# VectorE and ScalarE programs of a decode-attention kernel written as hardware loops

## The chip, the cores and the metric

The kernel runs on one core of a Trainium2 chip. The metric is the device time of one execution in microseconds (us), the median over the runs of a kernel. With each experiment the kernel before was run again on the same chip, in the same rounds. A ratio is the mean time of one kernel's runs over the mean of the other's runs of the same rounds, so it is not quite the ratio of the medians quoted beside it. The rounds ran on several chips; the kernel before took 1281.5 to 1281.8 us (medians) on each, so differences of under 0.3 us between rounds are not read.

In the profile PE stands for TensorE (PEld for its weight loads), DVE for VectorE, ACT for ScalarE, POOL for GpSimd and SP for SyncE; q1, q8 and q14 are queues of the sixteen DMA engines.

## The reference, cut to what matters

One token attends to a cache of 65,536 keys and values in each of eight key/value heads; two query heads share one of them. A small token-mixing network runs beside it, and a gate mixes both results.

```python
# x: [1, 1, 448];  k_cache, v_cache: [1, 8, 65536, 256] bf16, 268 MB each
q = (x @ wq).reshape(1, 1, 16, 256)...
scores = einsum("bhqd,bhkd->bhqk", q, repeat(k_cache, 2)) * 256 ** -0.5
o = einsum("bhqk,bhkd->bhqd", softmax(scores), repeat(v_cache, 2))
a = o.reshape(1, 1, 4096) @ wo
b = ...            # layernorm, outer product with w1, gelu, product with w2: 14 parts
return g * a + (1 - g) * b
```

Each byte of the caches is used once, for two query heads. Reading 537 MB is most of the work.

## The kernel before

Keys and values come in loads of 4 MB, alternately K and V, into a ring of four slots (two for K, two for V). One load holds four chunks of 2048 positions. SyncE issues a load when its slot has been read:

```python
def load(i):
    w, cd = loads[i]                       # ("k", 0), ("k", 1), ("v", 0), ("k", 2), ("v", 1), ...
    slot = slot_of(w, cd)
    if cd >= 2:
        if w == "k": eng.wait_ge(sem_tr, NB * DC * (cd - 1))     # K slot transposed
        else:        eng.wait_ge(sem_pv, DC * (cd - 1))          # V slot multiplied
    eng.dma_start(ring[:, slot]..., cache_src(w, cd)).then_inc(sem_in[slot], 16)
```

For each chunk TensorE transposes K into four PSUM banks, VectorE copies banks 0 and 2 to SBUF and ScalarE banks 1 and 3, TensorE makes scores, ScalarE their exponentials, and TensorE multiplies them with V. TensorE already runs in two hardware loops, with the network's product and the projection of seven heads between them. VectorE and ScalarE are written out (unrolled) over all 256 chunks:

```python
# TensorE
bodies(2, MID)                 # hardware loop, two load pairs per iteration
...                            # product of the network, projection of 7 heads
bodies(MID, NCD)               # a second copy of the same loop body

# VectorE: straight-line code for 256 chunks
for c in range(NC):
    cd, r = divmod(c, DC)
    if c >= KTB: vec.wait_ge(sem_qk, c - KTB + 1)
    if r == 0 and cd >= 2:
        vec.wait_ge(sem_pv, DC * (cd - 1))
        fold(cd - 2)...                            # add the load pair's sums to accs
        if (cd - 1) % (NCPH // DC) == 0: heads_den(...); heads_out(...)
    ...                                            # at MID: the results of the projection
    if c % BODY == 0 and c:
        vec.wait_ge(sem_qk, c)
        vec.tensor_copy(qcur[:, :, :], head_of(c)).then_inc(sem_qa, 16)
    for b in range(0, NB, 2):
        vec.wait_ge(sem_tr, NB * c + b + 1)
        vec.tensor_copy(ktT[:, c % KTB, b, :], kst_b[:, b, :]).then_inc(sem_ev[b], 1)
    ...                                            # 14 parts of the network in the first 19 chunks

# ScalarE: straight-line code for 256 chunks
for c in range(NC + 1):
    ...                                            # waits, two bank copies, one exponential
```

The softmax here doesn't subtract the row's maximum and nothing guards it: scores larger than these inputs give would overflow.

## Time and profile before

| | before |
|---|---|
| median time | 1281.62 us (3 runs, 1281.35 to 1282.36) |
| moved from HBM | 544.22 MB |
| instruction fetches in the span | 21 of 8 KB (q14), 18 of 16 KB (q8) |
| rate, 20 us windows of the steady part | about 433 GB/s |

These are lines of the page of the kernel before: the busy time of the engines; the 40-slice view (DMA in tenths busy, and GB/s); the DMA queues (packets, MB, share of sixteen engines); the chain of waits by engine; two groups of instructions (busy us, mean ns, then idle before and its cause); and the K loads (KB each, us from issue to landing).

```profile
span 1279.3 us, 45177 instructions
...
PE 1041.8 (81%) x20958; PEld 1024.3 (80%) x20958; DVE 425.9 (33%) x808; ACT 535.5 (42%) x786; POOL 0.9 (0%) x7
...
DMA  9999999999999999999999999999999999999996
GB/s 408 411 426 432 430 432 433 429 432 433 431 431 433 430 432 433 430 432 433 430 430 435 429 433 432 430 432 433 429 433 433 428 434 432 430 433 429 430 431 256
...
q1 hardware_dynamic: 21330, 544.22, 99.1%
q8 instruction: 18, 0.29, 0.1%
q14 instruction: 21, 0.17, 0.0%
...
DMA 61%; PE 33%; DVE 3%; issue 2%; ACT 1%; DVEq 0%; ACTq 0%; SPq 0%
...
L602 ACT ACTIVATE ktT<-kst 128x1024 bf16<-128x1024 bf16 x512 | 504.0, 1023 | 704.2 <-PE kst L255 703.6
L255 PE MATMUL kst<-ident,ring 128*128 128x128 f32 x4096 | 623.3, 321 | 209.2 <-DMA ring<-in_A_k_cache_dram 191.6
...
ring<-in_A_k_cache_dram SPq DMA_DIRECT2D x64, 4096.0 KB, 27.8
```

No compute engine is busy throughout (TensorE, the busiest, 81%). A K load takes 27.8 us from issue to landing although 4.19 MB at 433 GB/s need 9.7 us: about two other loads stand before it in the queue, so TensorE may be late without starving the queue.

The chain of waits, in order of time (start, us, what):

```profile
1252.20 22.02 DMA ring<-in_A_v_cache_dram
...
1274.27 0.60 PE acc L288 x16
...
1277.11 0.67 DVE out_b L566
```

TensorE starts its last 16 products only when the last piece of V is complete, at 1274.2 us, and all that follows is serial. The timeline has the same wait (start, us, what, and idle before):

```profile
1274.27 0.58 PE L288 MATMUL acc<-pT,ring 128*128 128x2 bf16 x16 [0.48 <-DMA ring<-in_A_v_cache_dram]
```

TensorE is idle for only 0.48 us there, for it is late itself: it had waited 3.88 us for the last K load, complete at 1254.7 us. What makes one engine end almost ten us after the first ones (their parts of this last piece are complete from 1264.7 us on, the last at 1274.2) is the subject of this study; the prediction below read past it.

Lines of TensorE (transposes) and ScalarE in a steady chunk, from the timeline (start, us, engine, line, what, and idle before), show the cadence of 2.59 us per chunk:

```profile
226.34 1.95 PE L255 MATMUL kst<-ident,ring 128*128 128x128 f32 x16
...
227.51 1.94 ACT L602 ACTIVATE ktT<-kst 128x1024 bf16<-128x1024 bf16 x2 [0.66 <-PE kst L255]
...
228.93 1.95 PE L255 MATMUL kst<-ident,ring 128*128 128x128 f32 x16
```

### The profile page before, as it was taken

How to read it: one execution, taken by the hardware profiler on the slowest of the kernel's cores; microseconds unless marked ns; L12 is line 12 of the kernel's file. 1: busy time of each engine (PE TensorE's matmuls, PEld its weight loads, DVE VectorE, ACT ScalarE, POOL GpSimd, SP SyncE). 2: the span in 40 equal slices, each digit the busy share in tenths (PEclk: the TensorE clock that was granted, in tenths of full speed). 3: DMA queues.
4: the chain of work that ended last, by engine and by line, in shares of the span. 5: the costliest groups of instructions: out<-in, count | busy, mean ns of one | idle time of the engine just before them, and what ended most of it. 6: DMA issues, size and time to landing. Idle time of an engine off the chain costs nothing.

```text
span 1279.3 us, 45177 instructions
## 1 busy us (share of the span) xinstructions
PE 1041.8 (81%) x20958; PEld 1024.3 (80%) x20958; DVE 425.9 (33%) x808; ACT 535.5 (42%) x786; POOL 0.9 (0%) x7
## 2 busy tenths in 40 slices
PE   4788987887877978878878778778788787789887
PEld 4777987887877877878878778778788787787887
DVE  3676332332332322323323223223233232232332
ACT  2454553443443533534434335335344343353452
POOL 0000000000000000000000000000000000000000
PEclk9778876877877777768778677777687786778876
DMA  9999999999999999999999999999999999999996
GB/s 408 411 426 432 430 432 433 429 432 433 431 431 433 430 432 433 430 432 433 430 430 435 429 433 432 430 432 433 429 433 433 428 434 432 430 433 429 430 431 256
DMA packets 21381, 544.70 MB, mean 426 GB/s; under 512 B 2264, under 2 KB 4315, under 8 KB 4702
## 3 DMA queue, kind: packets, MB, share of 16 engines
q1 hardware_dynamic: 21330, 544.22, 99.1%
q8 instruction: 18, 0.29, 0.1%
q14 instruction: 21, 0.17, 0.0%
q10 hardware_dynamic: 12, 0.01, 0.0%
HBM read 544.22 MB, written 0.00 MB: 425 GB/s over the span
## 4 chain that ended last, share of the span: by engine, by line
DMA 61%; PE 33%; DVE 3%; issue 2%; ACT 1%; DVEq 0%; ACTq 0%; SPq 0%
DMA ring<-in_A_k_cache_dram 59%; PE kst L255 25%; PE sps L267 5%; PE acc L288 2%; DMA ring<-in_A_v_cache_dram 2%; DMA b_b<-in_B_b_dram 1%; DVE ktT L534 0%; PE acc L324 0%; ACT zring L587 0%; PE acc L381 0%; DVE zring L462 0%; DVE wtmp L460 0%; DVE zring L466 0%; DVE gu L478 0%; DVE uring L458 0%
## 5 line engine op out<-in xcount | busy, mean ns | idle before, releaser
L602 ACT ACTIVATE ktT<-kst 128x1024 bf16<-128x1024 bf16 x512 | 504.0, 1023 | 704.2 <-PE kst L255 703.6
L255 PE MATMUL kst<-ident,ring 128*128 128x128 f32 x4096 | 623.3, 321 | 209.2 <-DMA ring<-in_A_k_cache_dram 191.6
L255 PEld LDWEIGHTS kst<-ident,ring 128*128 128x128 f32 x4096 | 578.4, 169 | 216.3 <-issue 104.3
L534 DVE COPY ktT<-kst 128x1024 bf16<-128x1024 bf16 x512 | 352.6, 691 | 512.7 <-PE kst L255 495.9
L267 PE MATMUL sps<-qcur,ktT 128*128 128x2 bf16 x8192 | 241.9, 163 | 3.8 <-DVE ktT L534 2.0
L267 PEld LDWEIGHTS sps<-qcur,ktT 128*128 128x128 bf16 x8192 | 238.7, 97 | 7.0 <-issue 2.2
L288 PE MATMUL acc<-pT,ring 128*128 128x2 bf16 x8192 | 228.7, 164 | 6.3 <-issue 5.8
L288 PEld LDWEIGHTS acc<-pT,ring 128*128 128x128 bf16 x8192 | 220.2, 99 | 6.6 <-issue 6.0
L501 DVE TENSOR_TENSOR accs<-accs,acc 128x36 f32<-128x36 f32 x55 | 10.6, 192 | 261.8 <-PE acc L288 261.7
L593 ACT ACTIVATE pT<-sps 128x32 bf16<-128x32 f32 x256 | 52.1, 203 | 6.6 <-PE sps L267 6.6
L275 PE MATMUL acc<-pT,ones_sq 128*128 128x32 bf16 x252 | 15.8, 176 | 0.0
L500 DVE COPY accs<-acc 128x36 f32<-128x36 f32 x8 | 1.6, 195 | 34.0 <-PE acc L288 33.9
L342 PE MATMUL acc<-ones_sq,gu 1*128 1x1 bf16 x42 | 1.3, 161 | 13.2 <-DMA b_b<-in_B_b_dram 13.2
L342 PEld LDWEIGHTS acc<-ones_sq,gu 1*128 1x128 bf16 x42 | 1.2, 99 | 13.2 <-DMA b_b<-in_B_b_dram 13.2
L275 PEld LDWEIGHTS acc<-pT,ones_sq 128*128 128x128 bf16 x252 | 10.7, 96 | 0.0
L587 ACT ACTIVATE zring<-zring 128x448 bf16<-128x448 bf16 x14 | 8.1, 577 | 6.2 <-DVE zring L468 6.1
L460 DVE TENSOR_TENSOR wtmp<-uring 128x448 bf16<-128x448 bf16 x14 | 5.5, 392 | 1.3 <-issue 0.3
L462 DVE TENSOR_TENSOR zring<-wtmp,uring 128x448 bf16<-128x448 bf16 x14 | 5.5, 393 | 1.0
L478 DVE TENSOR_TENSOR gu<-wtmp,zring 128x448 bf16<-128x448 bf16 x14 | 5.5, 392 | 1.0
L466 DVE TENSOR_TENSOR zring<-uring,wtmp 128x448 bf16<-128x448 bf16 x14 | 5.5, 392 | 1.0
L579 ACT ACTIVATE statb<-statb 1x1 bf16<-1x1 bf16 x1 | 0.2, 207 | 13.0 <-DVE statb L432 13.0
L324 PE MATMUL acc<-wo_sb,oTn 128*1 128x448 bf16 x28 | 5.5, 352 | 0.0
(75 smaller groups left out, 73.3 us busy)
## 6 DMA issues: line engine op xcount, KB each, us to landing
ring<-in_A_k_cache_dram SPq DMA_DIRECT2D x64, 4096.0 KB, 27.8
ring<-in_A_v_cache_dram SPq DMA_DIRECT2D x63, 4096.0 KB, 32.7
wo_sb<-in_A_wo_dram SPq DMA_DIRECT2D x8, 448.0 KB, 25.0
wo_sb<-in_A_wq_dram SPq DMA_DIRECT2D x1, 3072.0 KB, 19.2
ring<-in_A_v_cache_dram SPq DMA_DIRECT2D x1, 2048.0 KB, 18.4
ring<-in_A_v_cache_dram SPq DMA_DIRECT2D x1, 1024.0 KB, 20.5
ring<-in_A_v_cache_dram SPq DMA_DIRECT2D x2, 512.0 KB, 21.6
wo_sb<-in_A_wq_dram SPq DMA_DIRECT2D x1, 512.0 KB, 20.0
```

What stands on the lines that cost most here:

```text
L255: ins = pe.transpose(kst[:, b, j * P:(j + 1) * P], ring_f[:, slot, r * NT + 4 * b + j, :], ident[:, :])
L267: ins = pe.matmul(sps[:, par, 2 * nt:2 * nt + 2], ktT[:, par, b, ntl * DH + dj:(ntl + 1) * DH:2], qcur[:, dj, :], start=(dj == 0), stop=(d ...
L275: ins = pe.matmul(dst[:, DENC:NACC], ones_sq[:, :], pT[:, DC * par + r, :], start=(r == 0), stop=(r == DC - 1))
L288: ins = pe.matmul(acc[:, par, col:col + REP], ring[:, slot_of("v", par), n, dj:DH:2], pT[:, DC * par + r, 2 * nt:2 * nt + 2], start=(last ...
L324: ins = pe.matmul(dst[0:1, PRC:PRC + DM], oTn[:, g, j:j + 1], wo_sb[:, g, hh, dj * DM:(dj + 1) * DM], start=(first and hh == 0 and dj == 0 ...
L460: vec.tensor_tensor(W, U, U, op=ALU.mult)
L462: vec.tensor_tensor(Z, W, U, op=ALU.mult)
L501: return vec.tensor_tensor(dst, dst, src, op=ALU.add)
L534: vec.tensor_copy(ktT[:, c % KTB, b, :], kst_b[:, b, :]).then_inc(sem_ev[b], 1)
L587: act.activation(zring[:, slot, :], zring[:, slot, :], AF.Tanh).then_inc(s_tanh, 1)
L593: act.activation(pT[:, c % PTB, :], sps[:, c % 2, 0:2 * NT], AF.Exp, scale=scale).then_inc(sem_exp, 1)
L602: act.activation(ktT[:, c % KTB, b, :], kst_b[:, b, :], AF.Copy).then_inc(sem_ev[b], 1)
```

## The change

The intent is a smaller program: VectorE runs a loop over the heads with a loop over pairs of load pairs inside it, ScalarE a loop over eight chunks. Waits compare with register values, and head slices are addressed by register. To make the body the same in each iteration, one accumulator is cleared after each head instead of two in turn; the transposes get one semaphore per bank; a head is finished after the load pair, not ahead of its copies; and at the projection TensorE waits for VectorE's reading of the accumulator bank.

```diff
-            for c in range(NC):                    # VectorE
-                ...
+            for cd in range(0, HL, 2):             # first head, with the network: written out
+                pair(DC * cd, per_chunk=early)
+            pair(NCPH, next_head=1)
+            finish_head(0)
+            with nc.Fori(1, H - 1, 1, engines=on) as g:
+                with nc.Fori(0, 3, 1, engines=on) as m:
+                    pair(vec.snap(g * NCPH + m * BODY + BODY, ...))
+                pair(vec.snap(g * NCPH + NCPH, ...), next_head=g + 1)
+                finish_head(g)
+            ...                                    # results of the projection
+            with nc.Fori(DC * MID, NC, BODY, engines=on) as c0:
+                pair(c0)
...
-            for c in range(NC + 1):                # ScalarE
-                ...
+            for c in range(HEAD):                  # 24 chunks written out
+                chunk(c % BODY, c)
+                ...
+            with nc.Fori(HEAD, NC, BODY, engines=OrderedEngineSet([act.engine])) as c0:
+                for k in range(BODY):
+                    chunk(k, c0 + k)
...
-            pe.wait_ge(s_fold, 2)                  # TensorE, at the projection
+            pe.wait_ge(s_brow, 1)
             for g in range(H - 1):
-                ins = project(acc[:, 0, :], g, g == 0, g == H - 2)
+                ins = project(acc[:, 1, :], g, g == 0, g == H - 2)
             ins.then_inc(s_proj, 1)
+            pe.wait_ge(s_brow, 2)
```

As compiled, VectorE's program shrinks from 86,144 to 39,808 bytes and ScalarE's from 84,608 to 13,696. TensorE's stays at 281 KB.

More of the change, by code (lines that the diff above doesn't have):

```diff
@@ L76, in bass_gated_mix__gqa_block_cached__mixer_token_mlp__decode_kernel @@
     MID = NCD - 6
-    assert B0 + FT + 4 < DC * MID and MID >= (H - 1) * NCPH // DC + 2 and MID % 2 == 0
+    assert B0 + FT + 4 < DC * MID and MID == (H - 1) * NCPH // DC + 2
+    assert B0 + FT + 2 <= NCPH
     POC = 0
@@ L118, in bass_gated_mix__gqa_block_cached__mixer_token_mlp__decode_kernel @@
         oTn = sb([P, H, 2 * REP], bf16, "oTn")
-        accs = sb([P, 2, NACC], f32, "accs")
+        accs = sb([P, NACC], f32, "accs")
         part = sb([P, 2, REP], f32, "part")
-        rden = sb([P, 2, 2], f32, "rden")
-        densum = sb([P, 2, 2], f32, "densum")
+        rden = sb([P, REP], f32, "rden")
+        densum = sb([P, REP], f32, "densum")
         xrow_b = sb([1, DM], bf16, "xrow_b")
@@ L156, in bass_gated_mix__gqa_block_cached__mixer_token_mlp__decode_kernel @@
         sem_ident = new_sem("sem_ident")
-        sem_tr = new_sem("sem_tr")
+        sem_tr = [new_sem("sem_tr%d" % b) for b in range(NB)]
         sem_ev = [new_sem("sem_ev%d" % b) for b in range(NB)]
@@ L175, in bass_gated_mix__gqa_block_cached__mixer_token_mlp__decode_kernel @@
         s_bmm = new_sem("s_bmm")
-        s_fold = new_sem("s_fold")
+        s_brow = new_sem("s_brow")
         s_den = new_sem("s_den")
@@ L203, in load @@
                     if w == "k":
-                        eng.wait_ge(sem_tr, NB * DC * (cd - 1))
+                        eng.wait_ge(sem_tr[NB - 1], DC * (cd - 1))
                     else:
@@ L256, in transposes @@
                                            ring_f[:, slot, r * NT + 4 * b + j, :], ident[:, :])
-                    ins.then_inc(sem_tr, 1)
+                    ins.then_inc(sem_tr[b], 1)
             def scores(r, c):
@@ L378, in _ @@
             pe.wait_ge(s_pb, FT)
-            pe.wait_ge(s_fold, 1)
+            pe.wait_ge(sem_acc[1], 16 * (MID // 2))
             for kt in range(FT):
@@ L478, in b_partB, with heads_den @@
                 vec.tensor_tensor(gu[:, kt, :], W, TT, op=ALU.mult).then_inc(s_pb, 1)
-            def heads_den(g):
+            def heads_den():
                 vec.drain()
-                vec.reduce_sum(densum[:, g % 2, :],
-                               accs[:, g % 2, DENC:NACC].rearrange("p (nn hh) -> p hh nn", hh=REP),
+                vec.reduce_sum(densum[:, :], accs[:, DENC:NACC].rearrange("p (nn hh) -> p hh nn", hh=REP),
                                axis=AX.X)
                 vec.drain()
-                vec.reciprocal(rden[:, g % 2, :], densum[:, g % 2, :])
@@ L488, in heads_out @@
-            def heads_out(g):
-                po_v = accs[:, g % 2, POC:POC + 2 * REP].rearrange("p (dj hh) -> p dj hh", dj=2, hh=REP)
-                o_v = oTn[:, g, :].rearrange("p (dj hh) -> p dj hh", dj=2, hh=REP)
-                r_v = rden[:, g % 2:g % 2 + 1, :].broadcast_to((P, 2, REP))
-                vec.drain()
-                vec.tensor_tensor(o_v, po_v, r_v, op=ALU.mult).then_inc(s_oTn, 1)
-            def fold(cd):
-                g, k = divmod(cd, NCPH // DC)
-                vec.drain()
-                dst, src = accs[:, g % 2, :], acc[:, cd % 2, 0:NACC]
-                if k == 0:
-                    return vec.tensor_copy(dst, src)
-                return vec.tensor_tensor(dst, dst, src, op=ALU.add)
@@ L503, in head_of @@
-            def head_of(c):
-                return qT[:, :, REP * (c // NCPH):REP * (c // NCPH) + REP]
-            for c in range(NC):
-                cd, r = divmod(c, DC)
-                if c >= KTB:
-                    vec.wait_ge(sem_qk, c - KTB + 1)
-                if r == 0 and cd >= 2:
-                    vec.wait_ge(sem_pv, DC * (cd - 1))
-                    held = cd - 2 in (MID - 3, MID - 2)
-                    fold(cd - 2).then_inc(s_fold if held else sem_acc[cd % 2], 1 if held else 16)
-                    if (cd - 1) % (NCPH // DC) == 0:
-                        heads_den((cd - 2) // (NCPH // DC))
-                        heads_out((cd - 2) // (NCPH // DC))
-                if r == 0 and cd == MID:
-                    vec.wait_ge(s_bmm, 1)
-                    vec.tensor_copy(brow1[:, :], acc[0:1, 1, PRC:PRC + DM]).then_inc(sem_acc[1], 16)
-                    vec.drain()
-                    vec.tensor_scalar(brow[:, :], brow1[:, :], stat[:, 5:6], None, op0=ALU.add)
-                    vec.drain()
-                    vec.tensor_scalar(run[:, :], brow[:, :], stat[:, 6:7], None, op0=ALU.mult)
-                    vec.wait_ge(s_proj, 1)
-                    vec.drain()
-                    vec.scalar_tensor_tensor(run[:, :], acc[0:1, 0, PRC:PRC + DM], stat[:, 4:5],
-                                             run[:, :], op0=ALU.mult, op1=ALU.add).then_inc(sem_acc[0], 16)
-                if c % BODY == 0 and c:
-                    vec.wait_ge(sem_qk, c)
-                    vec.tensor_copy(qcur[:, :, :], head_of(c)).then_inc(sem_qa, 16)
-                for b in range(0, NB, 2):
-                    vec.wait_ge(sem_tr, NB * c + b + 1)
-                    vec.tensor_copy(ktT[:, c % KTB, b, :], kst_b[:, b, :]).then_inc(sem_ev[b], 1)
@@ new lines, in heads_den, with by_head, fold @@
+                vec.reciprocal(rden[:, :], densum[:, :])
+                vec.drain()
+            def by_head(out_v):
+                po_v = accs[:, POC:DENC].rearrange("p (dj hh) -> p dj hh", dj=2, hh=REP)
+                r_v = rden[:, :].rearrange("p (o hh) -> p o hh", o=1).broadcast_to((P, 2, REP))
+                return vec.tensor_tensor(out_v, po_v, r_v, op=ALU.mult)
+            def fold(par):
+                vec.drain()
+                return vec.tensor_tensor(accs[:, :], accs[:, :], acc[:, par, 0:NACC], op=ALU.add)
@@ new lines, in evacuate, with pair @@
+            def evacuate(r, c):
+                if not isinstance(c, int) or c >= KTB:
+                    vec.wait_ge(sem_qk, c - 1)
+                for b in range(0, NB, 2):
+                    vec.wait_ge(sem_tr[b], c + 1)
+                    vec.tensor_copy(ktT[:, r % KTB, b, :], kst_b[:, b, :]).then_inc(sem_ev[b], 1)
+            def pair(c0, next_head=None, per_chunk=None):
+                for par in range(2):
+                    if not isinstance(c0, int) or c0 >= BODY:
+                        vec.wait_ge(sem_pv, c0 + DC * par - DC)
+                        fold(par).then_inc(sem_acc[par], 16)
+                    if par == 0 and next_head is not None:
+                        vec.wait_ge(sem_qk, c0)
+                        vec.tensor_copy(qcur[:, :, :], qT[:, :, bass.ds(next_head * REP, REP)]
+                                        ).then_inc(sem_qa, 16)
+                    elif par == 0 and (not isinstance(c0, int) or c0):
+                        vec.sem_inc(sem_qa, 16)
+                    for r in range(DC):
+                        c = c0 + DC * par + r
+                        evacuate(r, c)
+                        if per_chunk is not None:
+                            per_chunk(c)
@@ L535, in _, with finish_head, early @@
+            def finish_head(g):
+                heads_den()
+                by_head(oTn[:, bass.ds(g, 1), :].rearrange("p o (dj hh) -> p (o dj) hh", hh=REP)
+                        ).then_inc(s_oTn, 1)
+                vec.drain()
+                vec.memset(accs[:, :], 0.0)
+            def early(c):
                 if c == 1:
@@ L538, in _ @@
                     vec.drain()
-                    vec.tensor_copy(qcur[:, :, :], head_of(0)).then_inc(sem_qa, 16)
+                    vec.tensor_copy(qcur[:, :, :], qT[:, :, 0:REP]).then_inc(sem_qa, 16)
                     vec.wait_ge(s_h, 1)
@@ L546, in _ @@
                     b_partA(c - B0)
-            g = (H - 1) % 2
+            vec.memset(accs[:, :], 0.0)
+            HL = NCPH // DC
+            on = OrderedEngineSet([vec.engine])
+            for cd in range(0, HL, 2):
[4 more added lines that the diff above has]
+                with nc.Fori(0, 3, 1, engines=on) as m:
+                    pair(vec.snap(g * NCPH + m * BODY + BODY, min_val=BODY, max_val=NC))
+                pair(vec.snap(g * NCPH + NCPH, min_val=BODY, max_val=NC), next_head=g + 1)
+                finish_head(g)
+            vec.wait_ge(s_bmm, 1)
+            vec.tensor_copy(brow1[:, :], acc[0:1, 1, PRC:PRC + DM]).then_inc(s_brow, 1)
+            vec.drain()
+            vec.tensor_scalar(brow[:, :], brow1[:, :], stat[:, 5:6], None, op0=ALU.add)
+            vec.drain()
+            vec.tensor_scalar(run[:, :], brow[:, :], stat[:, 6:7], None, op0=ALU.mult)
+            vec.wait_ge(s_proj, 1)
+            vec.drain()
+            vec.scalar_tensor_tensor(run[:, :], acc[0:1, 1, PRC:PRC + DM], stat[:, 4:5],
+                                     run[:, :], op0=ALU.mult, op1=ALU.add).then_inc(s_brow, 1)
+            with nc.Fori(DC * MID, NC, BODY, engines=on) as c0:
+                pair(c0)
             vec.wait_ge(sem_pv, NC - DC)
-            fold(NCD - 2)
+            fold(0)
             vec.wait_ge(s_den, 1)
             vec.drain()
-            vec.tensor_tensor(accs[:, g, DENC:NACC], accs[:, g, DENC:NACC], sps[:, 0, DENC:NACC], op=ALU.add)
-            heads_den(H - 1)
-            po_v = accs[:, g, POC:DENC].rearrange("p (dj hh) -> p dj hh", dj=2, hh=REP)
-            vec.drain()
-            vec.tensor_tensor(part[:, :, :], po_v, rden[:, g:g + 1, :].broadcast_to((P, 2, REP)), op=ALU.mult)
+            vec.tensor_tensor(accs[:, DENC:NACC], accs[:, DENC:NACC], sps[:, 0, DENC:NACC], op=ALU.add)
+            heads_den()
+            by_head(part[:, :, :])
             vec.wait_ge(sem_pv, NC)
@@ L560, in _ @@
                 ins = vec.scalar_tensor_tensor(oTn[:, H - 1, hh:2 * REP:REP], acc[:, 1, POC + hh:DENC:REP],
-                                               rden[:, g, hh:hh + 1], part[:, :, hh],
+                                               rden[:, hh:hh + 1], part[:, :, hh],
                                                op0=ALU.mult, op1=ALU.add)
@@ L587, in b_tanh, with weights, chunk @@
                 act.activation(zring[:, slot, :], zring[:, slot, :], AF.Tanh).then_inc(s_tanh, 1)
-            def weights(c):
+            def weights(par, c):
                 act.wait_ge(sem_qk, c + 1)
-                if c >= PTB:
+                if not isinstance(c, int) or c >= PTB:
                     act.wait_ge(sem_pv, c - PTB + 1)
-                act.activation(pT[:, c % PTB, :], sps[:, c % 2, 0:2 * NT], AF.Exp, scale=scale
+                act.activation(pT[:, par, :], sps[:, par % 2, 0:2 * NT], AF.Exp, scale=scale
                                ).then_inc(sem_exp, 1)
-            for c in range(NC + 1):
-                if c < NC:
-                    if c >= KTB:
-                        act.wait_ge(sem_qk, c - KTB + 1)
-                    for b in range(1, NB, 2):
-                        act.wait_ge(sem_tr, NB * c + b + 1)
-                        act.activation(ktT[:, c % KTB, b, :], kst_b[:, b, :], AF.Copy).then_inc(sem_ev[b], 1)
-                if c >= 1:
-                    weights(c - 1)
+            def chunk(k, c):
+                if not isinstance(c, int) or c >= KTB:
+                    act.wait_ge(sem_qk, c - 1)
+                for b in range(1, NB, 2):
+                    act.wait_ge(sem_tr[b], c + 1)
+                    act.activation(ktT[:, k % KTB, b, :], kst_b[:, b, :], AF.Copy).then_inc(sem_ev[b], 1)
+                if not isinstance(c, int) or c >= 1:
+                    weights((k - 1) % PTB, c - 1)
+            HEAD = 3 * BODY
+            for c in range(HEAD):
+                chunk(c % BODY, c)
                 if 0 <= c - B0 - 1 < FT:
                     b_tanh(c - B0 - 1)
+            with nc.Fori(HEAD, NC, BODY, engines=OrderedEngineSet([act.engine])) as c0:
+                for k in range(BODY):
+                    chunk(k, c0 + k)
+            weights(PTB - 1, NC - 1)
 _INS = ['A_x', 'A_k_cache', 'A_v_cache', 'A_wq', 'A_wo', 'B_x', 'B_w1', 'B_b1', 'B_w2', 'B_b2', 'gate_w']
```

## The prediction

> **What bounds it now.** DMA bandwidth. The page's 40-slice view gives DMA "9" in all but the last slice, at 429 to 435 GB/s nearly throughout; the queue table gives 544.22 MB and 99.1% of sixteen engines' span. The Trainium skill ("Advanced Engine Details and Errata", DMA Bandwidth Details) states 16 engines of 27.2 GB/s, 435 GB/s together; this trace agrees within 1% (433 in most 20 us windows). 544.22 MB at 433 GB/s is 1257 us. The other 24 us are the start (377 GB/s in the first 20 us, 413 to 419 in 40 to 80 us while wo loads run: about 5 us lost), the tail after the last V piece (5 us from 1274.3) and small drops. The chain of waits agrees: from 137 us on it alternates a K load of about 28 us with about 10 us of TensorE.
>
> **Slack.** A K load needs 9.7 us of bandwidth (4.19 MB at 433 GB/s) but lands a median 27.8 us after its issue: about two other loads are ahead of it. So TensorE may free a K slot some 15 us later before the queue runs dry. Each load pair takes 19.4 us, of which TensorE idles about 3.6 us waiting for K. Inside a chunk (2.59 us) ScalarE is busy 2.15 us (1.02 + 0.92 + 0.20) and VectorE 1.4 us; a bank is evacuated about 0.9 us before TensorE needs it.
>
> **What the change does.** Same loads, matmuls and evacuations. VectorE and ScalarE programs shrink; the instruction queue with 21 fetches (0.17 MB) should lose perhaps 10 of 8 KB: 0.1 MB, 0.2 us. Added: register arithmetic and branches. In TensorE's existing loop an ALU operation takes 32 ns and 10 serve one iteration; a compare-and-branch has a median of 208 ns and once 3.9 us (the skill, same page, Control Flow Timing, states about 108 ns; here it is longer). I estimate 3 to 5 register operations per chunk on each engine, 0.1 to 0.2 us, plus less run-ahead because a register operation can carry a wait: ScalarE's chunk could reach 2.4 to 2.6 us, about TensorE's cadence. If the cadence slips by 0.1 us, that is 0.8 us per 38.8 us, out of 7.2 us of TensorE idle time. Loop heads add 0.2 us, or 1 to 4 us if code is fetched again, per 8 chunks: still idle time.
>
> One memset per head replaces a copy; the head's division comes later, with no reader before the projection. There TensorE now waits also for VectorE's final read of acc (0.7 us): about 1 us more on a 10 us insertion that cost no bandwidth before (426 to 435 GB/s around 1160 us), so it is absorbed. Start and tail keep their order; [...] VectorE's last copies end 4 us before the last V piece lands.
>
> **Prediction.** None of the added work is on the DMA path: 1281.5 us, 8 in 10 between 1278.5 and 1286. Faster by over 2%: 1%. Within 2%: 95%. Slower by over 2%: 4%.
>
> **What would show it.** Right: GB/s slices unchanged, DMA about 99%, smaller instruction queue, K loads landing within 1 to 2 us of 27.8, TensorE's wait for K shorter by what its wait for evacuations grows. Wrong: GB/s falling in the steady slices, time to landing near 10 us, TensorE waiting mostly for ScalarE or VectorE.
>
> **What would make it wrong.** Register waits costing over 0.5 us per chunk on ScalarE, delaying TensorE by over 1 us per chunk; instruction fetches behind the bulk DMA at every iteration, over 7 us in 38.8; a stall at the very end.

## More of the kernel before

The DMA engines are busy everywhere except in the last slice.

The view by windows shows it closer. Its columns are length, busy us of the five engines with their counts, TensorE clock, DMA share, GB/s:

```profile
core 0: us, PE busy (x) PEld busy (x) DVE busy (x) ACT busy (x) POOL busy (x), PEclk, DMA share, GB/s
...
1264.00:1267.00 3.00, 3.00 (x74) 2.99 (x73) 1.39 (x2) 2.43 (x5) 0.00 (x0) 1.00 0.65 268
1267.00:1270.00 3.00, 3.00 (x125) 3.00 (x122) 0.00 (x0) 0.20 (x1) 0.00 (x0) 0.89 0.20 83
1270.00:1274.00 4.00, 3.79 (x142) 3.70 (x139) 0.90 (x5) 0.00 (x0) 0.00 (x0) 0.50 0.09 35
```

Times 16, the DMA share says that about ten engines were busy from 1264 to 1267 us, about three from 1267 to 1270 and about one from 1270 to 1274. The sixteen engines don't end together.

## The result, and the profile after

The kernel after took 1276.64 us (median of 4 runs, 1276.52 to 1276.66) against 1281.53 us before in the same rounds: 4.9 us less, ratio 0.996 (95% interval 0.9943 to 0.9978). That is within 2%, as forecast, but below the stated range, whose low end was 1278.5. The same lines of the page after:

```profile
span 1274.9 us, 45407 instructions
...
PE 1043.8 (82%) x20958; PEld 1025.4 (80%) x20958; DVE 425.3 (33%) x792; ACT 535.8 (42%) x786; POOL 0.9 (0%) x7
...
DMA  9999999999999999999999999999999999999997
GB/s 404 414 425 432 431 432 430 433 433 431 431 432 435 430 431 433 434 430 431 432 435 430 431 431 435 430 432 430 435 431 430 431 436 431 430 430 436 426 430 307
...
q1 hardware_dynamic: 21330, 544.22, 99.4%
q8 instruction: 18, 0.29, 0.1%
q14 instruction: 8, 0.07, 0.0%
...
DMA 61%; PE 33%; DVE 3%; issue 2%; ACT 1%; DVEq 0%; ACTq 0%; SPq 0%
...
L620 ACT ACTIVATE ktT<-kst 128x1024 bf16<-128x1024 bf16 x512 | 504.5, 1023 | 700.2 <-PE kst L256 699.3
L256 PE MATMUL kst<-ident,ring 128*128 128x128 f32 x4096 | 624.2, 322 | 203.8 <-DMA ring<-in_A_k_cache_dram 183.5
...
ring<-in_A_k_cache_dram SPq DMA_DIRECT2D x64, 4096.0 KB, 27.6
```

The GB/s line is the same within its scatter, up to the last slice, which has 307 instead of 256. The queue q14 has 8 fetches instead of 21. TensorE, ScalarE and the K loads' time to landing (27.6 us) hardly moved. So the middle of the kernel didn't get visibly faster. The windows at the end:

```profile
core 0: us, PE busy (x) PEld busy (x) DVE busy (x) ACT busy (x) POOL busy (x), PEclk, DMA share, GB/s
...
1264.00:1267.00 3.00, 3.00 (x122) 3.00 (x119) 0.39 (x3) 0.14 (x1) 0.00 (x0) 0.71 0.62 255
1267.00:1270.00 3.00, 2.67 (x100) 2.58 (x98) 0.51 (x3) 0.00 (x0) 0.00 (x0) 0.50 0.16 60
1270.00:1274.00 4.00, 2.04 (x19) 0.64 (x16) 1.02 (x3) 0.00 (x0) 0.00 (x0) 0.50 0.00 0
```

From 1264 to 1270 us there are again about ten and then two to three engines, but after 1270 us none. The chain's end:

```profile
1247.78 21.97 DMA ring<-in_A_v_cache_dram
...
1269.80 0.60 PE acc L289 x16
...
1272.64 0.67 DVE out_b L585
```

The last piece of V was issued 4.4 us earlier (1247.78 against 1252.20 us) and took the same 22 us; the last products start 4.5 us earlier, and the rest follows unchanged.

The trace records each increment of a semaphore by a DMA. The Trainium skill ("DMA: Bandwidth & Descriptors", Why a DMA increments its semaphore by 16 and not by 1) says that the engines of one DMA finish independently and that each adds one; the trace agrees, with 16 increments at different times for each load. So the trace tells for each load how far the last of the sixteen engines was behind their median:

| load complete near | before | after |
|---|---|---|
| 150 us | 2.1 us | 2.0 us |
| 300 us | 2.4 us | 2.5 us |
| 500 us | 3.3 us | 2.5 us |
| 700 us | 5.3 us | 2.5 us |
| 900 us | 6.2 us | 2.6 us |
| 1100 us | 7.2 us | 2.7 us |
| 1240 us | 6.6 us | 2.3 us |

Before, one engine falls behind in steps of 1 us; after, none does between 300 and 1100 us. (One such step is left, near 1183 us. From about 1180 us on the median engine is set back too, so the lag over it no longer shows every step.) The steps come with fetches of the queue q14. A packet of 32 KB takes a median of 1.216 us in this trace. In the steady part of before, fetches on q14 come in two kinds. Eight that take 0.31 to 0.32 us, at 187, 308, 440, 561, 681, 812, 934 and 1065 us, are each followed on the same DMA engine by a packet of 1.59 us, so the engine loses about 0.32 + 0.38 = 0.70 us. Others take 0.325 us (at 833 and 990 us, for instance) and are followed by one of 1.87 us: 0.325 + 0.65 = 0.98 us. That is the height of the steps. (In the trace an engine's packets follow each other within about 12 ns, so that the packet behind a fetch can be found by its start.)

### The profile page after: what moved, and what is told of

The parts are those of the page before. It is cut to its first block, busy times and chain, and to the rows that moved or that the text cites. A ratio compares the mean times of both kernels' runs of the same rounds, so it can differ in the third digit from the quotient of the medians. Undisturbed runs are those within 1.5% of the kernel's fastest.

```text
span 1274.9 us, 45407 instructions
## 1 busy us (share of the span) xinstructions
PE 1043.8 (82%) x20958; PEld 1025.4 (80%) x20958; DVE 425.3 (33%) x792; ACT 535.8 (42%) x786; POOL 0.9 (0%) x7
## 4 chain that ended last, share of the span: by engine, by line
DMA 61%; PE 33%; DVE 3%; issue 2%; ACT 1%; DVEq 0%; ACTq 0%; SPq 0%
DMA ring<-in_A_k_cache_dram 58%; PE kst L256 25%; PE sps L268 5%; PE acc L289 2%; DMA ring<-in_A_v_cache_dram 2%; DMA b_b<-in_B_b_dram 1%; DVE ktT L504 1%; PE acc L325 0%; PE acc L382 0%; ACT zring L606 0%; DVE zring L464 0%; DVE zring L468 0%; DVE wtmp L462 0%; DVE uring L460 0%; DVE wtmp L458 0%
## 5 line engine op out<-in xcount | busy, mean ns | idle before, releaser
L256 PE MATMUL kst<-ident,ring 128*128 128x128 f32 x4096 | 624.2, 322 | 203.8 <-DMA ring<-in_A_k_cache_dram 183.5
## 6 DMA issues: line engine op xcount, KB each, us to landing
ring<-in_A_k_cache_dram SPq DMA_DIRECT2D x64, 4096.0 KB, 27.6
```

What stands on the lines that cost most here:

```text
L256: ins = pe.transpose(kst[:, b, j * P:(j + 1) * P], ring_f[:, slot, r * NT + 4 * b + j, :], ident[:, :])
```

## The experiments

**Theory A, fetch lag.** A block of instructions is fetched by a DMA on one of the sixteen engines that also carry the caches. The blocks of one compute engine go through the same DMA engine. Each sets this engine back by 0.7 to 1 us, the delays add up, the ring of load slots hides them until the end, and the kernel ends with the last DMA engine. **B**: the gain comes from the restructured VectorE program. **C**: only the total of fetched bytes counts (0.1 MB, 0.2 us), which is how the prediction costed them. **D**: the loops change the pace of the engines.

### Which loop pays

The first three kernels are the kernel after with loops written out again, and nothing else undone:

```diff
-            with nc.Fori(1, H - 1, 1, engines=on) as g:           # VectorE: e1, e3
-                with nc.Fori(0, 3, 1, engines=on) as m:
-                    pair(vec.snap(g * NCPH + m * BODY + BODY, ...))
+            for g in range(1, H - 1):
+                for m in range(3):
+                    pair(g * NCPH + m * BODY + BODY)
...
-            with nc.Fori(DC * MID, NC, BODY, engines=on) as c0:
+            for c0 in range(DC * MID, NC, BODY):
...
-            with nc.Fori(HEAD, NC, BODY, engines=...) as c0:      # ScalarE: e1, e2
+            for c0 in range(HEAD, NC, BODY):
```

Both written out:

> The kernel after, with all loops of VectorE and ScalarE written out again and nothing else undone (the new order of folds, the memset per head, the wait at the projection stay). Theory A, fetch lag: each block of 8 KB of VectorE's instructions is fetched through one and the same DMA engine and sets that engine back by about 1 us, and the last of the sixteen engines ends the kernel; so the time returns to before: 1281 to 1282 us, with 19 to 22 instruction fetches on the small instruction queue. Rival B, the gain comes from the restructured VectorE program (fold, head, projection): 1276.6 us as after. Rival C, only the total bytes count (0.1 MB at 433 GB/s): 1276.9 us.

VectorE in loops, ScalarE written out:

> VectorE in loops, ScalarE written out. Theory A: VectorE's engine no longer lags; now the DMA engine that carries ScalarE's fetches (about 0.7 us each) is last. In the trace of before it was second, 2.9 us ahead of the last: so 1278.7 us (1278 to 1279.5). Rival C: about 1276.8. Rival B: 1276.6.

ScalarE in loops, VectorE written out:

> ScalarE in loops, VectorE written out. Theory A: the DMA engine with VectorE's fetches is last as before, nothing is won: 1281 to 1282 us, although 9 of the 13 saved fetches are ScalarE's. Rival C (bytes): most of the gain stays, 1276.8. Rival D (the loops' register waits change the pace of ScalarE): 1276.6 to 1279.

| kernel | time, us (5 runs) | ratio to before | fetches on q14 | lag of the last engine near 1100 us |
|---|---|---|---|---|
| before, same rounds | 1281.56 | | 21 | 7.2 us (first trace) |
| e1, both written out | 1281.30 | 0.9998 | 21 | 7.05 us |
| e2, VectorE in loops | 1278.42 | 0.9976 | 16 | 4.5 us |
| e3, ScalarE in loops | 1281.30 | 0.9998 | 13 | 7.3 us |

These are the q14 lines of e1, e2 and e3, in this order (packets, MB, share of sixteen engines), one fence each:

```profile
q14 instruction: 21, 0.17, 0.0%
```

```profile
q14 instruction: 16, 0.13, 0.0%
```

```profile
q14 instruction: 13, 0.11, 0.0%
```

All three results lie where theory A put them. B falls with e1: the restructured program, written out, is as slow as before. C, at whatever price per byte, falls with e2 and e3 together: e3 drops 8 of the 13 fetches and wins nothing, e2 drops 5 and wins 3.1 us. D falls for ScalarE with e3: its loop alone changes nothing. For VectorE, whose loop and fetches go together in e2, the runs do not separate D; against it stand the cadence of a chunk, the same before and after (2.59 and 2.58 us), and the lag, which grows at the fetches. In e2 the DMA engine with ScalarE's fetches comes last: its lag grows from 1.3 us near 500 us, where another engine is still the last with 2.4 us, to 4.5 us near 1100 us, 0.65 us for each of five fetches. This is why VectorE's loop alone wins 3.1 of the 4.9 us; the other 1.8 us come only when ScalarE's fetches go too. In e3 the lag grows from 2.36 us (load complete at 267.8 us) to 7.28 us (at 1147 us) over VectorE's five fetches at 367, 526, 685, 840 and 996 us: 0.98 us each.

The chain ends accordingly. The last piece of V (start, us) in e2 and then in e3:

```profile
1250.42 21.10 DMA ring<-in_A_v_cache_dram
```

```profile
1253.18 21.11 DMA ring<-in_A_v_cache_dram
```

### Fetches that nobody waits for

In the kernel after, GpSimd has nothing to do but make two constants. Here it also executes semaphore increments that no engine waits for.

```diff
             eng.memset(ones_sq[:, :], 1.0).then_inc(sem_ident, 1)
+            for _ in range(2048):                  # 4096 in the second kernel
+                eng.sem_inc(s_pad, 1)
```

> The kernel after, plus 2048 semaphore increments (nobody waits for them) on GpSimd, which is otherwise idle: 128 KB or 16 blocks more to fetch and not one more wait on the path. Theory A: if they all go through one DMA engine at 0.7 to 1.0 us each, less that engine's present lead of 0 to 5 us over the last one: +6 to +16 us, 1283 to 1293. Rival C: +0.3 us. Rivals B and D: no change.

> As the 16-block pad, with 4096 increments, 32 blocks of 8 KB. The 16 blocks cost 5.8 us over the kernel after. If each further block costs its engine 0.7 to 1.0 us and that engine is now alone at the end: +11 to +16 us over the 16-block run, 1294 to 1298 us. If the first 16 blocks' price was paid by something else (a collision in the first 165 us, say) or saturates: +0 to +6, 1282 to 1288.

The q14 lines of both:

```profile
q14 instruction: 24, 0.20, 0.0%
```

```profile
q14 instruction: 40, 0.33, 0.1%
```

The 16 blocks took the kernel from 1276.64 to 1282.40 us (4 runs), 5.8 us more, and 32 blocks to 1293.41 us (4 runs). The first step falls just short of the expected 6 us. Blocks 17 to 32 cost 11.0 us, 0.69 us each: the low end of the 11 to 16 us that were expected for them, and in total just under the range of 1294 to 1298 us. In the trace a GpSimd fetch of 0.309 us is followed by a packet of 1.566 us, 0.35 us over the median of 1.215 to 1.218: 0.66 us by this count. At that price the first 16 blocks would cost 10.6 us; they cost 5.8 because their engine was ahead of the last one at first (by about 4.8 us, an estimate from these two numbers). In aggregate bandwidth the 32 blocks are 0.26 MB, 0.6 us at 433 GB/s; they cost 16.8 us, because one engine of sixteen carries them and is also held up behind each.

Once the two constants are made, nothing in these kernels waits for GpSimd, and the arithmetic is the same. So it takes no stall of the engine that executes the instructions. That the fetches do it, and not the increments themselves, is read from the trace: only one DMA engine falls behind, by 0.65 to 0.66 us at each fetch (from 7.8 to 14.4 us over ten fetches between 137 and 241 us with 32 blocks). The windows of the 32-block kernel show what that looks like (its span is 1292.3 us):

```profile
1280.00:1288.00 8.00, 7.60 (x287) 7.44 (x283) 1.00 (x6) 0.37 (x3) 0.00 (x0) 0.68 0.06 24
```

Over 8 us a DMA share of 0.06: one engine of sixteen still working, the others done. In this kernel the ring does not hide the whole lag until the end: with 18 us of it, the rate is 401 to 417 GB/s from 280 to 380 us.

### TensorE's much larger program

TensorE's 281 KB are fetched in 16 KB blocks on the queue q8. If they too went through one engine, they would matter most. In e6 the first loop is split, so that one more copy of the body is fetched. In e7 there is a single loop, with the product and the projection under a branch:

```diff
-            bodies(2, MID)                         # e6
+            bodies(2, 30)
+            bodies(30, MID)
```
```diff
+                    with pe.If(cd == MID):         # e7, inside the one loop bodies(2, NCD)
+                        middle()
                     period(0, c0, u16, v16)
```

> The kernel after with TensorE's loop split once more (first 28 load pairs in one copy of the body, the next in another): 84 KB, 5 blocks of 16 KB more on the other instruction queue. If TensorE's blocks also went through one DMA engine, 5 times 1 to 2 us: 1280 to 1287. If they are spread over the engines, as the trace of the kernel after suggests (each late one on another engine): +0 to +1.5 us, 1276.6 to 1278.

> The kernel after with one TensorE loop over all load pairs; the projection stands under a branch on the loop's register inside it. 84 KB less of TensorE's code, 5 blocks fewer late in the kernel. Theory A with spread TensorE blocks: 0 to 1 us less, 1275.6 to 1276.6; if they share one engine: 1271 to 1274.

The q8 line of e6, then the q8 and q14 lines of e7 (after has 18 on q8 and 8 on q14):

```profile
q8 instruction: 24, 0.39, 0.1%
```

```profile
q8 instruction: 12, 0.20, 0.1%
q14 instruction: 8, 0.07, 0.0%
```

e6 took 1276.67 us and e7 1276.73 us (5 runs each): no change from 1276.64, with 24 or 12 TensorE blocks instead of 18. For e7, 0 to 1 us less had been expected. In e6 the late blocks lie on different engines as far as packets can be followed, and the lag of the last engine over the median falls from 2.46 us (near 620 us) to 1.8 us (near 900 us), as the median engine is delayed by the extra blocks and the last one is not. (It falls to 0.94 us; near 690 us an engine that a block has just hit becomes the last.) Spread over the engines, the blocks cost the kernel little; gathered on the engine that ends last, each counts in full. A single TensorE block can still decide which engine that is: in the kernel after, the fetch at 1231 us sets another engine back by about 1.6 us, and this one ends the kernel, 0.15 us behind VectorE's.

### Further along the same road

In e8 VectorE's loop over heads is rotated, so that it begins with a head's first pair and the last head needs no loop of its own; the projection's part stands under a branch. It builds on e7. VectorE's program goes to 35,136 bytes.

```diff
-            pair(NCPH, next_head=1)
-            finish_head(0)
-            with nc.Fori(1, H - 1, 1, engines=on) as g:
-                ...
+            with nc.Fori(1, H, 1, engines=on) as g:
+                pair(vec.snap(g * NCPH, ...), next_head=g)
+                finish_head(vec.snap(g - 1, ...))
+                with vec.If(g == H - 1):
+                    ...                            # results of the projection
+                with nc.Fori(0, 3, 1, engines=on) as m:
+                    pair(vec.snap(g * NCPH + m * BODY + BODY, ...))
```

> As the last, and VectorE's loop over heads rotated, so that the first head's end and the last head's pairs run in the same loop body (the projection's part under a branch): VectorE's program shrinks from 39.8 to 35.1 KB and nothing has to be fetched when the loop over heads is left. Theory A: one or two VectorE blocks fewer at about 1 us, then the next engines are last (1.6 us behind in the trace of the kernel after): 1274.5 to 1276. Rival B (control flow costs time): above 1276.6.

e8 took 1276.05 us (5 runs, 1275.48 to 1276.33; ratio to before 0.9954). In e7 the lag of the last engine steps from 2.76 to 3.75 us at VectorE's fetch at 1182 us, when it leaves its loop over heads. In e8 this fetch and this step are gone (7 fetches on q14), and 0.6 to 0.7 us are won. The expected 1 us didn't come in full, since the last engine was already 3.1 us behind near 300 us, against 2.7 us in e7.

e9 takes 42 instructions more out of the network's 14 parts:

```diff
-                vec.drain()                                                      # part A
...
-                vec.drain()                                                      # part B
                 vec.tensor_scalar(TT, TT, 1.0, None, op0=ALU.add)
-                vec.tensor_scalar(W, U, 0.5, None, op0=ALU.mult)
                 vec.drain()
-                vec.tensor_tensor(gu[:, kt, :], W, TT, op=ALU.mult).then_inc(s_pb, 1)
+                vec.scalar_tensor_tensor(gu[:, kt, :], U, 0.5, TT, op0=ALU.mult, op1=ALU.mult).then_inc(s_pb, 1)
```

> The last kernel (one loop body on TensorE and on VectorE) with VectorE's program cut by 42 instructions more, from 35.1 to 32.4 KB, just under four blocks of 8 KB (two pipeline drains less, and two multiplications in one instruction, in each of the 14 parts of the small network). Theory A: one VectorE block fewer than the last, its engine comes 1 us earlier and still ends 0.6 us behind the next one: 1275.0 us (1274.7 to 1275.4). If the fifth block is fetched all the same[...]: 1276.0. If the DMA engines no longer decide: 1276.

> The kernel after, unchanged, on the same chip and in the same rounds, so that differences under 1 us can be read: 1276.6 us.

e9 took 1275.49 us (5 runs, 1275.41 to 1275.83) and the kernel after, in the same rounds, 1276.63 us (1276.31 to 1276.81). Its range doesn't touch theirs, so e9 beats the kernels before and after, by 6.0 us and 1.1 us. It is correct. Its number lies between the two that were expected, and its reason is not the one given: the trace has as many blocks of 8 KB fetched within the span as e8's (7). The last engine is 2.3 us behind near 300 us instead of 3.1 in e8's trace, so this difference arises in the first 300 us. Why it does is open. That e9 is faster than e8 at all isn't shown: they ran on different chips, both have the ratio 0.9954 to before, e8's trace is of its slowest run (1276.33 us), and its two fastest runs (1275.48 and 1275.52 us) are as fast as e9's.

## Why the prediction was wrong

**The time.** 1281.5 us was forecast, 1278.5 to 1286; it was 1276.64. The class "within 2%" was right.

**The step that failed** is "the instruction queue with 21 fetches (0.17 MB) should lose perhaps 10 of 8 KB: 0.1 MB, 0.2 us". The number of fetches was close (13). The price was not: the bytes were divided by the rate of all sixteen engines, as if every fetch were spread over them. Five of the thirteen were VectorE's, all on the engine that ended the kernel, and they cost this engine 0.98 us each, 4.9 us. The other eight, ScalarE's, were worth nothing by themselves (e3), for their engine ended 2.8 us ahead (before: last piece complete at 1271.39 us on the second-last engine, 1274.22 us on the last). But with VectorE's five gone ScalarE's engine is the last (e2, 3.1 us won), and only with both gone were 4.9 us won. The term was too small by a factor of over 20, and it wasn't one term, but one per DMA engine with a maximum over them. (The sum of 4.9 us agrees with the time won more closely than it should: some 0.2 us of it lie outside the profiled span, for time minus span is about 2.0 us in the kernel before and 1.8 to 1.9 us in all the others, e1 included; and in the two traces the last piece of V lands 4.5 us earlier.)

**The bound** was right and too coarse. "DMA bandwidth" is the sum of sixteen engines, and the kernel ends with the slowest. The drop of the last slice to 256 GB/s stood on the page and was put down to the tail.

**The slack** was right. The K loads' time to landing went from 27.8 to 27.6 us, and TensorE's wait for K from 191.6 to 183.5 us in the list of waits; its wait for VectorE's copies from 13.7 to 14.8 us, so the two didn't offset each other as forecast. The same slack hides the lag of a single DMA engine until the end of the kernel.

**The cost of the loops** was put too high, without consequence. ScalarE executes 464 ALU operations of 35 ns in 232 looped chunks, two per chunk, and VectorE 294 of 40 ns in 216 looped chunks, 1.4 per chunk; 3 to 5 had been estimated. A compare-and-branch takes a median of 45 ns on ScalarE and 56 ns on VectorE, against 208 ns on TensorE, which the prediction had used. The Trainium skill ("Advanced Engine Details and Errata", Control Flow Timing) states about 108 ns. No loop fetches its body again at each iteration: there are 8 fetches in the whole span. The cadence of a steady chunk in the timeline after is as before (start to start 2.58 us):

```profile
226.03 1.95 PE L256 MATMUL kst<-ident,ring 128*128 128x128 f32 x16
...
227.14 1.94 ACT L620 ACTIVATE ktT<-kst 128x1024 bf16<-128x1024 bf16 x2 [0.56 <-PE kst L256]
...
228.61 1.95 PE L256 MATMUL kst<-ident,ring 128*128 128x128 f32 x16
```

**The projection.** About 1 us more on TensorE was forecast. It waits for VectorE twice now, 0.80 us before the projection and 1.47 us behind it, both times named in the timeline (idle before, in brackets):

```profile
1153.78 5.46 PE L325 MATMUL acc<-wo_sb,oTn 128*1 128x448 bf16 x28 [0.80 <-DVE xcb_row L558]
...
1159.36 0.67 DVE L565 SCALAR_TENSOR_TENSOR run<-acc,stat,run 1x448 f32<-1x448 f32 x1 [4.79 <-PE acc L325]
...
1160.71 3.77 PE L256 MATMUL kst<-ident,ring 128*128 128x128 f32 x32 [1.47 <-DVE run L565]
```

These 2.3 us cost no bandwidth (437 GB/s from 1140 to 1160 us in the view by windows), as forecast.

## What to carry to other kernels

When DMA is the bound, read the end of the kernel by DMA engine: if the DMA share decays in stairs over the last ten us, single engines may carry something that the others don't, as here, and total bytes over total rate will not show it. Instruction blocks are such a load. In straight-line code of VectorE, ScalarE or GpSimd each block of 128 instructions cost 0.7 to 1 us of one DMA engine here, even where nothing waited for the compute engine that runs them; but only the blocks on the DMA engine that ends last can be won back, so shrink that program first and look again. Here the next DMA engine ended only 2.8 us before it and had to be relieved too.

## What the Trainium skill lacked or had wrong

- "Runtime: NRT & Kernel Launch", Instruction fetch mechanics, calls the cost of crossing a block boundary "one DMA tail-bump, mostly hidden". No stall of the compute engine was needed here: each block delayed a DMA engine by 0.69 us (GpSimd, by the time of the kernels), 0.65 us (ScalarE, by the lag in e2; about 0.70 us by the packets) or 0.98 us (VectorE, by the lag), and 32 blocks that nobody waited for cost 16.8 us.
- The same section says that kernels "prefer full unrolling where possible". With the bulk DMA as the bound it was the reverse: 1281.3 us written out, 1276.6 us in loops.
- The same section gives blocks of 16 KiB. Here q14 (ScalarE, VectorE, GpSimd) fetched blocks of 8,192 bytes and q8 (TensorE) of 16,384.
- "DMA: Bandwidth & Descriptors", Queues, rings and completion order, says that row 14 is internal to the runtime and serves refills, which agrees with q14. TensorE's fetches came on q8 instead (18). It doesn't say how fetches are placed. Here all of ScalarE's could be followed to one DMA engine (9 in the trace of e1), VectorE's and GpSimd's each added up on one (5 steps of 0.98 us; 11.0 us for 16 blocks), and TensorE's, in e6, were spread as far as they could be followed.
- No page says that a fetch of 8 KB also lengthens the packet behind it: 1.59 us (ScalarE), 1.57 us (GpSimd) or 1.87 us (VectorE) against 1.22 us. Why it does, no run here shows.
- "Advanced Engine Details and Errata", Control Flow Timing, has one figure of about 108 ns for a compare-and-branch; the medians here were 45 ns (ScalarE), 56 ns (VectorE) and 208 ns (TensorE).
